# A shorter lead-in and the last weights rounded earlier, in a fused attention and mixer kernel

## The chip, the cores and the metric

The kernel runs on one core of a Trainium2 chip. A core has five engines that run side by side[...]: TensorE (PE, matrix products and transposes), VectorE (DVE), ScalarE (ACT), GpSimd (POOL) and SyncE (SP), which here only issues transfers. Data come from HBM by DMA into SBUF; TensorE writes its results to PSUM. The metric is the device time of one execution in microseconds, the median of the runs.

## The reference

Attention in which a query sees only the keys of its own cluster, and behind it an MLP mixer, in float32:

```python
# q, k, v: (4, 8, 768, 64); centroids: (8, 16, 64)
q_n, k_n, c_n = q / |q|, k / |k|, centroids / |centroids|      # norms + 1e-6
q_assign = argmax(q_n @ c_n.T);  k_assign = argmax(k_n @ c_n.T)
mask   = q_assign[:, :, :, None] == k_assign[:, :, None, :]
scores = where(mask, q @ k.T / 8, -1e9)
attn   = softmax(scores) @ v
x  = attn.transpose(0, 2, 1, 3).reshape(4, 768, 512)
u  = x + (relu(x^T @ w_tok1) @ w_tok2)^T      # over the tokens: 768 -> 256 -> 768
out = u + relu(u @ w_ch1) @ w_ch2             # over the channels: 512 -> 1536 -> 512
```

## The kernel before

The heads are worked on in 16 pairs (`g`), each in six iterations (`m`), 96 in all. While pair `g` is computed, the clusters of pair `g + 1` are found (the routing): `q` and `k` are turned in blocks of 32, multiplied by the normed centroids, turned back, compared with their maximum, and the one-hot rows turned into `ohT`. The product of the one-hots is added to the scores in PSUM and does the masking.

The lead-in does all that for pair 0, with nothing beside it:

```python
def centroids_norm(cen):
    ...                                     # ss = sum of squares, lo = max(ss, 2**-100)
    nrm = small.tile([P, 1], F32, name="nrm0")
    nc.scalar.sqrt(nrm, lo)                 # L243
    for it in range(2):                     # two Newton steps, L246 to L252
        ... reciprocal, scalar_tensor_tensor, tensor_scalar on VectorE
    ...                                     # reciprocal, scaling (cn), turn on TensorE (pc),
                                            # copies to cnT and cnd (L257 to L267)

def begin():
    cen = small.tile([P, D], F32, name="cen")
    nc.sync.dma_start(cen, centroids.rearrange("h c d -> (h c) d"))
    load(0, (nc.scalar, nc.sync))           # q issued by ScalarE, k by SyncE; four transfers each
    make_identity(nc, ident)
    ...
    load(1)
    centroids_norm(cen)
    turn(0)                                 # two 128x768 turns on VectorE, k then q (L276)
    route_products(0)                       # pr, four f32 products of q and k together (L287)
    route(0)                                # sim, mx, oh on VectorE (L301 to L307)
    for a in (1, 0):
        route_turn(0, a)                    # six turns on TensorE, copy to ohT by ScalarE
```

A float32 product stands in the trace as two matmul records; that is why `pr` has eight.

The weights are rounded in steps. A step takes one piece of up to 128x512 and has two operations on ScalarE, three on VectorE and an integer addition on GpSimd; transfer, ScalarE's part and the rest of a piece lie in three steps that follow each other:

```python
def scalar_part(p):
    nc.scalar.activation(out=p["h"]..., in_=p["hi"]..., func=ACT.Abs)              # L193
    nc.scalar.activation(out=p["up"], in_=p["lo"], func=ACT.Copy, scale=2.0**-29)  # L195
def rest(dst, p):
    nc.vector.tensor_scalar(...)            # L200, max and min
    nc.vector.tensor_scalar(...)            # L205, mask and shift
    nc.vector.scalar_tensor_tensor(...)     # L210
    nc.gpsimd.tensor_tensor(...)            # L217
```

The loop over the iterations, and what comes behind it:

```python
begin()
weights = list(weight_steps(stage, W, ("tok1", "tok2", "ch1")))
ends = [...]                                # 32 token products: tok1 (two per batch), tok2 (six)
for m in range(last + 5):                   # last = 96
    g, s = divmod(m, GROUPS)                # GROUPS = 6
    ...                                     # outputs, sums, scores, values of the pair
    if g < NPAIR - 1:
        ...                                 # the routing of pair g + 1, one part at each s
    if s == 1 and g + 2 < NPAIR:
        load(g + 2)
    if m % WEVERY == 0 and weights:         # WEVERY = 4
        weights.pop(0)()
    ...
    if m >= last:
        for _ in range(2):
            if ends:
                ends.pop(0)()               # ten of the 32
attention.close()
W["ch2"] = ...
beside = list(left_weights())               # four sums of 128x1536 on VectorE (w1s, L474)
beside += weight_steps(pool("mstage", 2, staging), W, ("ch2",))   # 12 pieces, 14 steps
while ends:                                 # the other 22
    for _ in range(-(-len(beside) // len(ends))):
        beside.pop(0)()
    ends.pop(0)()
    if len(ends) in (11, 9):
        turn_u(0, len(ends) == 9)           # turns x to uT; at 9 also four differences (uTs)
```

`tok2` writes a PSUM tile (four buffers in `ps_m`), and VectorE adds it to `x` and frees it:

```python
def tok2(b, j):
    pu = mtile([P, DM], "pu")
    for t in range(NT):
        nc.tensor.matmul(pu, lhsT=W["tok2"][:, t, j], rhs=h1s[b][:, t], ...)     # L460
    nc.vector.tensor_tensor(out=xs[b][:, j], in0=pu, in1=xs[b][:, j], op=ALU.add) # L463
```

Behind that come the channel products (L584 and L635, seven products in place of eight), which take the second half of the time.

Of the kernel before, what the change touches and what calls it, by code (L numbers as in the profile page):

```python
# [8 lines left out]
F32 = mybir.dt.float32  # L9
BF16 = mybir.dt.bfloat16  # L10
# [36 lines left out]
def kernel(  # L47
# [46 lines left out]
    wc1pool = pool("wc1pool", 1)  # L94
    tokens = fast.enter_context(ExitStack())
    tokpool = pool("tokpool", 1, tokens)
    attention = fast.enter_context(ExitStack())
    loads = pool("loads", 2, attention)
# [4 lines left out]
    stage = pool("stage", 2, attention)  # L103
    pools = {}


# [5 lines left out]
    ohs = [small.tile([P, 2, NJ, P], BF16, name=f"oh{i}", bufs=1) for i in range(2)]  # L112
    rcps = const.tile([P, 2 * NPAIR, 2, HJ], F32, name="rcps")
    cells = const.tile([P, NPAIR], F32, name="cells")

# [10 lines left out]
    def load(g, queues=None):  # L126


        b, f = divmod(g, NF)
        st = state.setdefault(g, {})  # L130
        st["qk"] = loads.tile([P, 2, NJ, NQ, QP], F32, name="qk")
        st["va"] = loads.tile([P, 2, NJ, D], F32, name="va", bufs=3)
# [99 lines left out]


    def centroids_norm(cen):
        sq = small.tile([P, D], F32, name="censq")
        ss = small.tile([P, 1], F32, name="ss")
# [3 lines left out]
        lo = small.tile([P, 1], F32, name="lo")  # L240
        nc.vector.tensor_scalar_max(out=lo, in0=ss, scalar1=float(2.0**-100))
        nrm = small.tile([P, 1], F32, name="nrm0")
        nc.scalar.sqrt(nrm, lo)  # L243
        for it in range(2):
            rr = small.tile([P, 1], F32, name="rr")
            nc.vector.reciprocal(out=rr, in_=nrm)  # L246
            tw = small.tile([P, 1], F32, name="tw")
# [3 lines left out]
            nrm = small.tile([P, 1], F32, name="nrm")  # L251
            nc.vector.tensor_scalar(  # L252
                out=nrm, in0=tw, scalar1=0.5, scalar2=(1e-6 if it else 0.0),
                op0=ALU.mult, op1=ALU.add,
            )
        rden = small.tile([P, 1], F32, name="rden")
        nc.vector.reciprocal(out=rden, in_=nrm)  # L257
        cn = small.tile([P, 2, D], F32, name="cn")
        for i in range(2):
            nc.vector.tensor_scalar_mul(out=cn[:, i], in0=cen, scalar1=rden)  # L260
        pc = ps_w.tile([P, H * C], F32, tag="w", name="pc")
        nc.tensor.transpose(out=pc, in_=cn.rearrange("p i d -> p (i d)"), identity=ident)
        nc.vector.tensor_copy(out=cnT, in_=pc)
        nc.vector.memset(cnd, 0.0)
        for i in range(2):
            rows = slice(i * D, (i + 1) * D)
            nc.vector.tensor_copy(  # L267
                out=cnd[rows, :, i], in_=cnT.rearrange("p (f i c) -> p f i c", f=NF, i=2)[rows, :, i]
            )


    def turn(g):
        st = state[g]
        st["T"] = qktp.tile([P, 2, NJ, P], F32, name="qkT")
        for a in (1, 0):
            nc.vector.transpose(  # L276
                out=st["T"][:, a].rearrange("p j t -> p (j t)"),
                in_=st["qk"][:, a].rearrange("p j i d -> p (j i d)"),
            )

    def route_products(g):

        st, f = state[g], g % NF
        pr = ps_w.tile([P, 2, NJ, QP], F32, tag="w", name="pr")
        for i in range(NQ):
            rows = slice(i * QP, (i + 1) * QP)
            nc.tensor.matmul(  # L287
                pr[rows], lhsT=cnd[:, f].rearrange("p i c -> p (i c)"),
                rhs=st["T"][:, :, :, rows].rearrange("p a j r -> p (a j) r"),
                start=True, stop=True,  # L290
            )
        st["pr"] = pr

    def route(g):

        st = state[g]
        NR = 2 * NJ * 2
        sc = small.tile([P, NR, C], F32, name="sim")  # L300
# [3 lines left out]
        mx = small.tile([P, NR], F32, name="mx")  # L304
        nc.vector.reduce_max(out=mx, in_=sc, axis=AX.X)
        oh = ohs[g % 2].rearrange("p a j (h x) -> p (a j) h x", h=2)[:, :, :, 0:C]
        nc.vector.tensor_tensor(  # L307
            out=oh, in0=sc.rearrange("p (n h) c -> p n h c", h=2),
            in1=mx.rearrange("p (n h) -> p n h", h=2).unsqueeze(3).to_broadcast([P, 2 * NJ, 2, C]),
            op=ALU.is_ge,  # L310
        )
# [167 lines left out]
    def left_weights():  # L479

        w = W["ch1"]
        half = DCH // 2
        A = {
            f"A{i + 1}{j + 1}": w[:, 2 * j : 2 * j + 2, half * i : half * i + half]
            for i in range(2)
            for j in range(2)
        }
        extra = pools["wsums"].tile([P, 3, 2, half], F32, name="w1s")
        A["S1"], A["S2"], A["S4"] = (extra[:, i] for i in range(3))
        yield lambda: add(A["S1"], A["A21"], A["A22"])  # L490
# [191 lines left out]


    def begin():
        cen = small.tile([P, D], F32, name="cen")
# [4 lines left out]
        nc.vector.memset(ones, 1.0)  # L690
# [7 lines left out]
        for a in (1, 0):  # L698
            route_turn(0, a)

    begin()
    weights = list(weight_steps(stage, W, ("tok1", "tok2", "ch1")))
# [12 lines left out]
    for m in range(last + 5):  # L715
# [37 lines left out]
    assert not weights and not state  # L753
    attention.close()
    other = fast.enter_context(ExitStack())
    W["ch2"] = pool("wc2pool", 1, other, side="right").tile([P, NCT, DM], F32, name="wc2")
    pools["wsums"] = pool("wsums", 1, other, side="right")
    pools["u"] = pool("upool", 1, other, side="right")
    staging = ExitStack()
# [238 lines left out]
```

## Time and profile before

| | |
|---|---|
| time, median of 3 runs | 924.56 us (924.08 to 924.62) |
| span of the profiled execution | 919.6 us |
| TensorE busy | 892.4 us, 97% |
| VectorE busy | 507.0 us, 55% |
| ScalarE busy | 309.6 us, 34% |
| first score product | 16.45 us after the start |
| first channel product (pX, L584) | 465.5 us after the start |

An engine's busy time is summed over its instructions. "PE" is the matmuls and "PEld" the loading of their stationary operand. A row of the timeline gives the start in us, the length, engine and line, operation, and tiles; what stands in brackets is the time that the engine was idle before, and what ended it. Busy shares are means over stages with different limits, so the stages are looked at one by one below.

### The profile page before, as it was taken

What the parts mean: (1) busy time and instruction counts of PE and PEld (TensorE: products, weight loads), DVE (VectorE), ACT (ScalarE), POOL (GpSimd) and SP (SyncE); (2) the same over time, 40 slices, a digit from 0 to 9 for tenths busy, and PEclk for the clock granted to TensorE, in tenths of its full rate; (3) what the DMA queues carried; (4) which work ended last, traced back from release to release, by engine and by line L of the source; (5) the groups of instructions that cost most, each with busy time, mean ns of one, the idle gap of its engine ahead of it and who ended that gap; (6) DMA issues with size and microseconds to landing.
All of it is one profiled execution on the core that took longest, in us unless ns stands there. A gap on an engine that the chain in (4) does not pass through costs nothing.

```text
span 919.6 us, 11532 instructions
## 1 busy us (share of the span) xinstructions
PE 892.4 (97%) x4563; PEld 524.2 (57%) x4563; DVE 507.0 (55%) x842; ACT 309.6 (34%) x517; POOL 48.5 (5%) x40
## 2 busy tenths in 40 slices
PE   4999999999999999999999899999999999999997
PEld 1444444444444444444457668677686776868676
DVE  4778787878787865147865344342443334433342
ACT  3565555656565555103521031210212112130210
POOL 1010100101010100002310000000000000000000
PEclk9999999999999999999999999999999999999999
DMA  8343435243434110002400000000010000100001
GB/s 173 75 99 84 92 77 110 66 110 84 96 87 76 43 48 1 1 0 75 132 0 1 1 0 35 35 0 1 1 46 23 1 1 0 58 12 1 0 13 60
DMA packets 112829, 41.74 MB, mean 45 GB/s; under 512 B 101632, under 2 KB 105728, under 8 KB 112768
## 3 DMA queue, kind: packets, MB, share of 16 engines
q1 hardware_dynamic: 109632, 40.55, 18.0%
q10 hardware_dynamic: 3136, 0.39, 0.3%
q8 instruction: 37, 0.61, 0.3%
q14 instruction: 24, 0.20, 0.1%
HBM read 34.64 MB, written 6.29 MB: 45 GB/s over the span
## 4 chain that ended last, share of the span: by engine, by line
PE 95%; DVE 3%; ACT 1%; issue 0%; ACTq 0%; DVEq 0%
PE sc L349 18%; PE av L378 15%; PE pX L635 14%; PE pX L584 14%; PE pZ L635 7%; PE pZ L584 7%; PE ph L451 5%; PE pY L635 3%; PE pY L584 3%; PE pu L460 3%; PE px L413 2%; PE po L325 2%; PE pr L287 1%; PE den L394 1%; PE pt L523 1%; DVE wh L200 1%
## 5 line engine op out<-in xcount | busy, mean ns | idle before, releaser
L355 ACT ACTIVATE ex<-sc 128x768 f32<-128x768 f32 x192 | 145.3, 808 | 117.2 <-PE sc L349 117.2
L368 DVE TENSOR_TENSOR sum<-sum,ex 128x768 f32<-128x768 f32 x128 | 133.5, 1043 | 30.6 <-ACT ex L355 22.2
L378 PE MATMUL av<-ex,va 128*64 128x384 f32 x768 | 145.1, 499 | 0.0
L349 PE MATMUL sc<-qkT 64*128 64x384 f32 x768 | 140.6, 485 | 0.0
L378 PEld LDWEIGHTS av<-ex,va 128*64 128x64 f32 x768 | 46.6, 136 | 86.5 <-issue 82.7
L349 PEld LDWEIGHTS sc<-qkT 64*128 64x128 f32 x768 | 71.2, 188 | 31.8 <-issue 0.6
L584 PE MATMUL pX<-uT,wc 128*128 128x384 f32 x192 | 67.4, 487 | 1.6 <-issue 1.6
L592 ACT COPY p<-pX 128x384 f32<-128x384 f32 x24 | 11.4, 475 | 143.2 <-PE pX L584 143.2
L584 PEld LDWEIGHTS pX<-uT,wc 128*128 128x128 f32 x192 | 36.2, 190 | 26.4 <-issue 2.7
L217 POOL TENSOR_TENSOR wc<-wT,wup 128x512 int32<-128x512 int32 x24 | 35.3, 1470 | 290.8 <-DVE wT L210 182.3
L349 PE MATMUL sc<-ohT 64*128 64x384 bf16 x384 | 48.5, 329 | 1.7 <-ACT ohT L327 1.0
L460 PE MATMUL pu<-h,wt 128*128 128x512 f32 x96 | 43.1, 596 | 3.6 <-DVE x L463 3.6
L419 DVE TENSOR_TENSOR x<-px,rcps 128x384 f32<-128x384 f32 x32 | 17.8, 558 | 49.4 <-PE px L413 47.9
L451 PE MATMUL ph<-x,wt 128*128 128x512 f32 x96 | 42.1, 594 | 0.0
L477 DVE TENSOR_TENSOR c<-pZ,u 128x384 f32<-128x384 f32 x24 | 13.4, 558 | 46.8 <-PE pZ L584 46.8
L477 DVE TENSOR_TENSOR x<-pX,x 128x256 f32<-128x256 f32 x24 | 10.2, 424 | 51.3 <-PE pX L635 51.3
L477 DVE TENSOR_TENSOR hA<-pY,p 128x384 f32<-128x384 f32 x24 | 13.4, 557 | 40.7 <-PE pY L584 40.7
L635 PE MATMUL pX<-w2s,hA 128*128 128x256 f32 x144 | 35.1, 380 | 0.5 <-DVE x L477 0.5
L635 PE MATMUL pX<-wc,hA 128*128 128x256 f32 x144 | 35.0, 379 | 0.0
L635 PE MATMUL pZ<-w2s,hS 128*128 128x256 f32 x144 | 35.0, 379 | 0.0
L635 PE MATMUL pY<-wc,hA 128*128 128x256 f32 x144 | 35.0, 379 | 0.0
L635 PE MATMUL pX<-w2s,hS 128*128 128x256 f32 x144 | 35.0, 379 | 0.0
(111 smaller groups left out, 1209.3 us busy)
## 6 DMA issues: line engine op xcount, KB each, us to landing
raw<-in_moe_w_ch_dram SPq DMA_DIRECT2D x24, 512.0 KB, 3.9
qk<-in_k_dram SPq DMA_DIRECT2D x64, 96.0 KB, 4.4
va<-in_v_dram SPq DMA_DIRECT2D x16, 384.0 KB, 3.4
out_dram<-x SPq DMA_DIRECT2D x24, 256.0 KB, 2.0
qk<-in_q_dram SPq DMA_DIRECT2D x60, 96.0 KB, 3.1
raw<-in_moe_w_tok_dram SPq DMA_DIRECT2D x3, 512.0 KB, 5.1
raw<-in_moe_w_tok_dram SPq DMA_DIRECT2D x4, 384.0 KB, 3.5
qk<-in_q_dram ACTq DMA_DIRECT2D x4, 96.0 KB, 3.6
```

The lines of the kernel that those rows point to most:

```text
L217: nc.gpsimd.tensor_tensor(out=dst.bitcast(I32), in0=T, in1=up, op=ALU.add)
L325: nc.tensor.transpose(out=po[:, j], in_=oh[:, a, j], identity=identb)
L349: nc.tensor.matmul(scs[i][:, h, 0:HS], lhsT=src[rows, 1, j0 + i], rhs=src[rows, 0, js], start=start, stop=not start,)
L355: nc.scalar.activation(out=ex, in_=scs[i][:, :, 0:HS], func=ACT.Exp, scale=SM_SCALE)
L368: nc.vector.tensor_tensor(out=acc, in0=acc, in1=e[i], op=ALU.add)
L378: nc.tensor.matmul(st["av"][h * D : (h + 1) * D], lhsT=st["va"][:, h, j], rhs=ex[:, h], start=(j == 0), stop=(j == NJ - 1),)
L413: nc.tensor.transpose(out=px[:, i], in_=avT[:, i], identity=ident)
L451: nc.tensor.matmul(pf, lhsT=W["tok1"][:, j, t * P : (t + 1) * P], rhs=xs[b][:, j], start=(j == 0), stop=(j == NJ - 1),)
L460: nc.tensor.matmul(pu, lhsT=W["tok2"][:, t, j], rhs=h1s[b][:, t], start=(t == 0), stop=(t == NT - 1))
L477: nc.vector.tensor_tensor(out=dst, in0=a, in1=b, op=ALU.add)
L584: nc.tensor.matmul(psum, lhsT=A[a][:, k, c * P : (c + 1) * P], rhs=R[r][:, k], start=start and k == 0, stop=k == 1, skip_group_check=not s ...
L635: nc.tensor.matmul(psum, lhsT=h2[a][:, k, i * P : (i + 1) * P], rhs=Bw[w][:, 3 * part + k], start=start and k == 0, stop=k == 2, skip_grou ...
```

## The change

It has two parts. The first is to shorten the lead-in. The root of the norms is computed on VectorE, from a first guess out of the bits and one more Newton step, so that ScalarE needs no table for it; the table of the exponential is loaded at once, by an exponential that nothing uses. `k` is turned and routed ahead of `q`, so that the engines overlap, and `q`'s one-hots of pair 0 are copied by VectorE. Matmuls of zeros, whose result nothing reads, keep TensorE at work between the real ones.

The second moves the rounding of the last weights (`ch2`) forward: it begins with the last pair of heads, whose iterations have no next pair to route, and takes the place in SBUF that the routing leaves. For that, the routing's tiles get pools of their own at the right end of SBUF. What is rounded, and how, stays the same.

The core of the diff (renamed pools and the loops that only pass on `a0`, `a1` are left out):

```diff
@@ centroids_norm
-        nrm = small.tile([P, 1], F32, name="nrm0")
-        nc.scalar.sqrt(nrm, lo)
-        for it in range(2):
+        nrm = rsmall.tile([P, 1], F32, name="nrm0")
+        nc.vector.tensor_scalar(
+            out=nrm.bitcast(I32), in0=lo.bitcast(I32), scalar1=0.5, scalar2=float(0x1FBD1DF5),
+            op0=ALU.mult, op1=ALU.add,
+        )
+        for it in range(3):
@@ turn, route_products, route: for one of k and q alone
-    def turn(g):
+    def turn(g, kinds=(1, 0)):
-    def route_products(g):
+    def route_products(g, a0=0, a1=2):
-    def route(g):
+    def route(g, a0=0, a1=2):
@@ route_turn
         if a == 0:
-            nc.scalar.copy(out=st["ohT"][:, 0], in_=po)
+            if g == 0:
+                nc.vector.tensor_copy(out=st["ohT"][:, 0], in_=po)
+            else:
+                nc.scalar.copy(out=st["ohT"][:, 0], in_=po)
@@ begin
         load(0, (nc.scalar, nc.sync))
+        nc.vector.memset(ones, 1.0)
+        warm = rsmall.tile([P, WMAX], BF16, name="warm")
+        nc.vector.memset(warm, 0.0)
+        nc.scalar.activation(out=rsmall.tile([P, QP], F32, name="expd"), in_=ones, func=ACT.Exp)
         make_identity(nc, ident)
         ...
         load(1)
+        pw = ps_av.tile([P, HS], F32, name="av")
+        def keep_warm(n):
+            for _ in range(n):
+                nc.tensor.matmul(pw, lhsT=warm[:, 0:P], rhs=warm[:, P : P + HS], start=True, stop=True)
+        keep_warm(12)
         centroids_norm(cen)
-        turn(0)
-        route_products(0)
-        route(0)
-        for a in (1, 0):
-            route_turn(0, a)
+        keep_warm(7)
+        turn(0, (1,))
+        route_products(0, 1, 2)
+        turn(0, (0,))
+        route(0, 1, 2)
+        keep_warm(1)
+        route_products(0, 0, 1)
+        keep_warm(2)
+        route_turn(0, 1)
+        route(0, 0, 1)
+        keep_warm(1)
+        route_turn(0, 0)
@@ the loop
-        if m % WEVERY == 0 and weights:
+        if m == last - GROUPS:
+            assert not weights
+            routing.close()
+            W["ch2"] = pool("wc2pool", 1, side="right").tile([P, NCT, DM], F32, name="wc2")
+            weights = list(weight_steps(stage, W, ("ch2",)))
+        if (m % WEVERY == 0 if m < last - GROUPS else m % 2 or m > last) and weights:
             weights.pop(0)()
@@ behind the loop
-    beside = list(left_weights())
-    beside += weight_steps(pool("mstage", 2, staging), W, ("ch2",))
+    beside = weights + list(left_weights())
```

More of the change, by code (lines that the diff above doesn't have):

```diff
@@ L96 @@
     tokpool = pool("tokpool", 1, tokens)
+    staging = fast.enter_context(ExitStack())
+    stage = pool("stage", 2, staging)
     attention = fast.enter_context(ExitStack())
-    loads = pool("loads", 2, attention)
+    loads = pool("loads", 3, attention)
     small = pool("small", 2, attention)
@@ L102 @@
     sums = pool("sums", 2, attention)
-    stage = pool("stage", 2, attention)
+    routing = fast.enter_context(ExitStack())
+    qkpool = pool("qkpool", 2, routing, side="right")
+    rsmall = pool("rsmall", 2, routing, side="right")
     pools = {}
@@ L111 @@
     cnd = const.tile([P, NF, 2, C], F32, name="cnd")
-    ohs = [small.tile([P, 2, NJ, P], BF16, name=f"oh{i}", bufs=1) for i in range(2)]
+    ohs = [rsmall.tile([P, 2, NJ, P], BF16, name=f"oh{i}", bufs=1) for i in range(2)]
     rcps = const.tile([P, 2 * NPAIR, 2, HJ], F32, name="rcps")
@@ L130, in load @@
         st = state.setdefault(g, {})
-        st["qk"] = loads.tile([P, 2, NJ, NQ, QP], F32, name="qk")
-        st["va"] = loads.tile([P, 2, NJ, D], F32, name="va", bufs=3)
+        st["qk"] = qkpool.tile([P, 2, NJ, NQ, QP], F32, name="qk")
+        st["va"] = loads.tile([P, 2, NJ, D], F32, name="va")
         for a, src in ((1, k), (0, q)):
@@ L234, in centroids_norm @@
     def centroids_norm(cen):
-        sq = small.tile([P, D], F32, name="censq")
-        ss = small.tile([P, 1], F32, name="ss")
+        sq = rsmall.tile([P, D], F32, name="censq")
+        ss = rsmall.tile([P, 1], F32, name="ss")
         nc.vector.tensor_tensor(out=sq, in0=cen, in1=cen, op=ALU.mult)
         nc.vector.reduce_sum(out=ss, in_=sq, axis=AX.X)
-        lo = small.tile([P, 1], F32, name="lo")
+        lo = rsmall.tile([P, 1], F32, name="lo")
         nc.vector.tensor_scalar_max(out=lo, in0=ss, scalar1=float(2.0**-100))
-        nrm = small.tile([P, 1], F32, name="nrm0")
-        nc.scalar.sqrt(nrm, lo)
-        for it in range(2):
-            rr = small.tile([P, 1], F32, name="rr")
+        nrm = rsmall.tile([P, 1], F32, name="nrm0")
[4 more added lines that the diff above has]
+        for it in range(3):
+            rr = rsmall.tile([P, 1], F32, name="rr")
             nc.vector.reciprocal(out=rr, in_=nrm)
-            tw = small.tile([P, 1], F32, name="tw")
+            tw = rsmall.tile([P, 1], F32, name="tw")
             nc.vector.scalar_tensor_tensor(
@@ L250, in centroids_norm @@
             )
-            nrm = small.tile([P, 1], F32, name="nrm")
+            nrm = rsmall.tile([P, 1], F32, name="nrm")
             nc.vector.tensor_scalar(
-                out=nrm, in0=tw, scalar1=0.5, scalar2=(1e-6 if it else 0.0),
+                out=nrm, in0=tw, scalar1=0.5, scalar2=(1e-6 if it == 2 else 0.0),
                 op0=ALU.mult, op1=ALU.add,
             )
-        rden = small.tile([P, 1], F32, name="rden")
+        rden = rsmall.tile([P, 1], F32, name="rden")
         nc.vector.reciprocal(out=rden, in_=nrm)
-        cn = small.tile([P, 2, D], F32, name="cn")
+        cn = rsmall.tile([P, 2, D], F32, name="cn")
         for i in range(2):
@@ L269, in centroids_norm @@
             )
-    def turn(g):
+    def turn(g, kinds=(1, 0)):
         st = state[g]
-        st["T"] = qktp.tile([P, 2, NJ, P], F32, name="qkT")
-        for a in (1, 0):
+        if 1 in kinds:
+            st["T"] = qktp.tile([P, 2, NJ, P], F32, name="qkT")
+        for a in kinds:
             nc.vector.transpose(
@@ L279, in turn @@
             )
-    def route_products(g):
+    def route_products(g, a0=0, a1=2):
         st, f = state[g], g % NF
-        pr = ps_w.tile([P, 2, NJ, QP], F32, tag="w", name="pr")
+        pr = ps_w.tile([P, a1 - a0, NJ, QP], F32, tag="w", name="pr")
         for i in range(NQ):
@@ L288, in route_products @@
                 pr[rows], lhsT=cnd[:, f].rearrange("p i c -> p (i c)"),
-                rhs=st["T"][:, :, :, rows].rearrange("p a j r -> p (a j) r"),
+                rhs=st["T"][:, a0:a1, :, rows].rearrange("p a j r -> p (a j) r"),
                 start=True, stop=True,
@@ L292, in route_products @@
         st["pr"] = pr
-    def route(g):
+    def route(g, a0=0, a1=2):
         st = state[g]
-        NR = 2 * NJ * 2
-        sc = small.tile([P, NR, C], F32, name="sim")
+        NR = (a1 - a0) * NJ * 2
+        sc = rsmall.tile([P, NR, C], F32, name="sim")
         nc.vector.transpose(
@@ L303, in route @@
         )
-        mx = small.tile([P, NR], F32, name="mx")
+        mx = rsmall.tile([P, NR], F32, name="mx")
         nc.vector.reduce_max(out=mx, in_=sc, axis=AX.X)
-        oh = ohs[g % 2].rearrange("p a j (h x) -> p (a j) h x", h=2)[:, :, :, 0:C]
+        oh = ohs[g % 2][:, a0:a1].rearrange("p a j (h x) -> p (a j) h x", h=2)[:, :, :, 0:C]
         nc.vector.tensor_tensor(
             out=oh, in0=sc.rearrange("p (n h) c -> p n h c", h=2),
-            in1=mx.rearrange("p (n h) -> p n h", h=2).unsqueeze(3).to_broadcast([P, 2 * NJ, 2, C]),
+            in1=mx.rearrange("p (n h) -> p n h", h=2).unsqueeze(3).to_broadcast([P, NR // 2, 2, C]),
             op=ALU.is_ge,
@@ L684, in begin @@
     def begin():
-        cen = small.tile([P, D], F32, name="cen")
+        cen = rsmall.tile([P, D], F32, name="cen")
         nc.sync.dma_start(cen, centroids.rearrange("h c d -> (h c) d"))
         load(0, (nc.scalar, nc.sync))
+        nc.vector.memset(ones, 1.0)
+        warm = rsmall.tile([P, WMAX], BF16, name="warm")
+        nc.vector.memset(warm, 0.0)
+        nc.scalar.activation(out=rsmall.tile([P, QP], F32, name="expd"), in_=ones, func=ACT.Exp)
         make_identity(nc, ident)
         nc.gpsimd.tensor_copy(out=identb, in_=ident)
-        nc.vector.memset(ones, 1.0)
         for oh in ohs:
@@ L693, in begin @@
         load(1)
-        centroids_norm(cen)
-        turn(0)
-        route_products(0)
-        route(0)
-        for a in (1, 0):
-            route_turn(0, a)
+        pw = ps_av.tile([P, HS], F32, name="av")
[3 more added lines that the diff above has]
+        keep_warm(12)
+        centroids_norm(cen)
+        keep_warm(7)
[10 more added lines that the diff above has]
+        route_turn(0, 0)
     begin()
@@ L752 @@
                     ends.pop(0)()
-    assert not weights and not state
+    assert not state
     attention.close()
[L755 to L759, printed above, removed]
-    beside = list(left_weights())
-    beside += weight_steps(pool("mstage", 2, staging), W, ("ch2",))
+    pools["wsums"] = pool("wsums", 1, side="right")
+    pools["u"] = pool("upool", 1, side="right")
+    beside = weights + list(left_weights())
     while ends:
```

## The prediction

> **What bounds the kernel now.** I first read the page's engine shares. TensorE is busy for 892.4 of 919.6 us, so the kernel can only get shorter where TensorE stands still or runs slowly. I then cut the span into stretches (the table by windows; its columns are the length, then busy time and instruction count of PE, PEld, DVE, ACT and POOL, the granted clock, the DMA share and GB/s):
> ```profile
> PE 892.4 (97%) x4563; PEld 524.2 (57%) x4563; DVE 507.0 (55%) x842; ACT 309.6 (34%) x517; POOL 48.5 (5%) x40
> ...
> 0.00:16.45 16.45, 3.42 (x22) 1.68 (x23) 8.54 (x24) 3.11 (x6) 3.62 (x9) 1.00 0.88 178
> 16.45:22.80 6.35, 5.68 (x33) 2.71 (x33) 1.44 (x2) 4.19 (x5) 0.00 (x0) 1.00 0.90 152
> 22.80:370.00 347.20, 347.20 (x2510) 152.94 (x2508) 263.10 (x379) 201.36 (x303) 29.55 (x19) 1.00 0.34 76
> 370.00:445.30 75.30, 75.30 (x218) 34.09 (x215) 35.71 (x50) 15.85 (x29) 8.22 (x7) 1.00 0.14 42
> 445.30:465.70 20.40, 16.76 (x39) 6.74 (x38) 19.37 (x27) 5.97 (x10) 7.11 (x6) 1.00 0.25 77
> ```
> TensorE is full from 22.8 to 445.3 us. It is nearly idle in the first 16.45 us, and it loses some of the stretch from 445.3 to 465.7 us, where VectorE is busy for 19.37 of 20.40 us. The change touches just these two places, so each is read by itself.
>
> For the first, the timeline (start, length, engine and line, operation, tiles; in brackets the idle time before it and what ended it), with the rows that carry the chain:
> ```profile
> 3.64 1.28 ACT L243 ACT_TABLE_LOAD   x1 [3.64 <-issue]
> 5.17 0.16 DVE L246 RECIPROCAL rr<-nrm 128x1 f32<-128x1 f32 x1 [2.02 <-ACT nrm L243]
> ...
> 7.21 0.45 PE L262 MATMUL pc<-ident,cn 128*128 128x128 f32 x1 [7.21 <-DVE cn L260]
> ...
> 8.59 1.84 DVE L276 STREAM_TRANSPOSE qkT<-qk 128x768 f32<-128x768 f32 x2
> ...
> 10.48 1.51 PE L287 MATMUL pr<-qkT,cnd 128*32 128x384 f32 x8 [2.82 <-DVE qkT L276]
> ...
> 17.04 2.52 PE L349 MATMUL sc<-qkT 64*128 64x384 f32 x8
> ...
> 20.62 1.47 PE L349 MATMUL sc<-qkT 64*128 64x384 f32 x8
> ```
> The reader is to see three things: VectorE waits 2.02 us for a root on ScalarE, whose table load cannot start until ScalarE has issued q's transfers; everything behind it is one serial chain (norms, turn, products, route, turn of the one-hots, scores); and the same eight score matmuls take 2.52 us at 17.04 and 1.47 us at 20.62.
>
> For the second, the chain that ended last, in order of time:
> ```profile
> 457.14 0.60 DVE x L463
> 457.74 1.11 DVE wh L200
> 458.86 0.02 issue
> 458.88 0.44 DVE wh L205
> 459.32 0.04 DVEq L210
> 459.35 0.04 issue
> 459.40 0.69 DVE wT L210
> 460.09 0.60 DVE x L463
> ```
> This cycle of 2.95 us (457.14 to 460.09) frees one PSUM tile. TensorE fills one with four tok2 matmul records at 0.43 us each (a run of 24 took 10.30 us), so in 1.72 us. VectorE is the bound here, because a step of rounding the ch2 weights stands between two additions. The waits put it so:
> ```profile
> PE pu L460 <- DVE x L463: 3.6, 4, 1.0
> ```
>
> **What the Trainium skill says.** "TensorE: Matmul & The Clock Gate", Part 1: The HAM clock gate, says that TensorE runs at half rate until it has been busy for a window of about 3.4 us, and falls back after an idle one. The trace fits the first half: 0.315 us a score matmul (2.52/8) becomes 0.18 (1.47/8) after some 3 us of dense work. The window table's granted clock shows 1.00 all through, so durations are the evidence, not that column. "ScalarE: Activation LUTs", What ACT_TABLE_LOAD costs, gives 1283 ns; the two loads here took 1.28 us each (at 3.64 and 16.41). "DMA: Bandwidth & Descriptors", Issuing engines are not separate DMA queues, says that transfers of all queues share the same engines. The DMA share of 0.88 in the lead-in agrees, and so I expect k, the second half of a shared burst, to land no earlier than now. "SBUF — State Buffer", Who interferes with whom, says that a VectorE scalar operation in its two-port mode and a GpSimd operation block each other. The trace agrees: the first weight operation (L200) takes 0.42 us when it runs free and 1.18 us when it starts beside GpSimd's 1.27 us addition, so one rounding step costs VectorE 1.54 to 2.3 us.
>
> **Part 1, the lead-in.** *Root on VectorE.* The norm's first operation ends at 3.15 us, as now. Removed: the wait from 3.15 to 5.17. Added: a first guess (0.18 with the gap, as the 128x1 operation L252) and a third iteration. An iteration goes from 5.17 to 5.81, so 0.64 us. The three end at 3.17 + 0.18 + 3 x 0.64 = 5.27, where the two now end at 6.45. The rest is unchanged in length: to the end of cn 0.63, to the copy of pc 0.62, to the end of cnd 0.89. VectorE is then free at 7.41 instead of 8.59.
>
> *A new wait for k.* k's last transfer is issued at 3.66 and lands after 4.0 us (the view of tile qk), at 7.66; the last of q lands at about 7.2. Neither changes. So the turn of k starts at about 7.75, and of the 1.18 us freed by the root only 0.84 is kept.
>
> *k ahead of q.* A turn of one of them takes 0.925 us: k 7.75 to 8.67, q 8.67 to 9.6. TensorE makes k's products (half of the eight) beside q's turn. The route of one half starts at 9.62. A 192-column transpose out of PSUM (tile dent) takes 0.38 us where the 384-column one takes 0.58, so I take 0.38, 0.36 and 0.38 for the three operations and 0.13 of gaps: 1.25 us. k's route ends at 10.85, q's at 12.1. k's six transposes and ScalarE's copy with its accumulator (0.81 + 0.19) run beside q's route and end by about 12.4. After q's route: six transposes 0.5, and a VectorE copy of 768 columns, which I estimate at 0.95 from the transpose of as many, with handovers 0.1. The first scores start at 13.65 instead of 16.45: 2.8 us less.
>
> *Table and dummy matmuls.* The exp table is loaded behind q's issues, and the load at 16.41 goes; it lay beside the 3.12 us of cold scores, so alone it brings nothing. A dummy matmul has 384 columns; by the cold spacing of the TensorE page (columns over 1.2 GHz) I estimate 0.32 us for it, so twelve take 3.8 us, from about 1.2 to 5.0. pc is wanted at 5.9, so they delay nothing. Seven more take 1.1 us (warm) to 2.2 (cold) from 6.5 on, and k's products are due at 8.7. If TensorE is warm at 13.65, the first scores take 1.9 us and not 3.1, and the second exponential ends 3.2 us after their start where it now takes 3.95 (16.45 to 20.40). The second scores follow it at once and their last part is warm already (20.45 to 22.08). That brings about 0.75 us more, with some 0.15 us for products and transposes.
>
> Sum for the lead-in: 2.8 + 0.9 = **3.7 us**. Behind it lies a stretch in which TensorE never waits, so it should be kept whole. The turn of pair 1 needs q of pair 1, which lands at 11.0 + 3.7 = 14.7; TensorE asks for its products only at 18.4, so this wait stays hidden.
>
> **Part 2, the last weights.** Fourteen steps move forward: seven into the last pair of heads and the iterations after it, seven to the first seven of the 22 remaining token products, and the four VectorE sums of w1s (1.75 us each) behind them. All are over with the eleventh of the 22, just where the first u is turned. In 445.3 to 465.7 VectorE keeps four uTs differences (445.32 to 449.68, 4.4 us) and additions of 0.69 us per tile. Four PSUM buffers cover 4 x 1.72 = 6.9 us, more than the 4.4, so TensorE should run through. From 445.34 it has 36 records x 0.43 = 15.5 us to do and now takes until 465.67, 20.3 us. Gain: **4.8 us**, which agrees with 3.6 us of waits plus four restarts at 0.26 (1.98 instead of 1.72).
>
> Does it cost anything where it goes? In the last pair a step falls on every second iteration of about 3.6 us. VectorE owes the sums 1.74 us per iteration (five of about 1.04 in three), the outputs and reciprocals about 0.4, and 0.8 to 1.15 for half a step: 3.0 to 3.3 us. Routing, 3.64 us in six iterations (turn 1.95, then 0.58, 0.55 and 0.56), is missing there. In the token products after it, the tightest run is six tok2 tiles with five steps and one sum: VectorE needs some 17 us where TensorE needs 10.3, but four buffers and then two long tok1 tiles (12 records, 5.15 us each) lie behind it; my count by hand leaves no wait.
>
> Total: 924.56 - 3.7 - 4.8 = 916.06, rounded to 916.0.
>
> **The rivals.** (a) *The lead-in is bound by transfers.* If k landed later, because the first transfers differ between executions or the other traffic moves up, nearly the whole gain of the root would be lost: about 917. For it: a DMA share of 0.88; against it: nothing in the order of the transfers changes. (b) *The clock stays cold.* The gaps between the dummies are about 1 us, so an interrupted run may not count as busy. Then 0.9 us is lost, and a cold pair of dummies stands in front of k's transposes: 917 to 917.3. (c) *VectorE stays the bound of the transition.* If the moved steps let VectorE fall behind before the turns of u, its backlog reaches the same additions and half of the 4.8 us comes back: about 918.5. For it: 17 us of work against 10.3; against it: the two long tiles, and that TensorE shows no wait in the similar stretch before 445. (d) *The last pair is held up.* ScalarE gets 1.34 us of weight work (0.67 + 0.66 us) in every second iteration beside two exponentials of 0.81; should it delay the exponentials, three such iterations lose 1 us together: 917.
>
> **Range and chances.** Each part alone could miss by about a third: 2.3 to 4.8 us for the lead-in and 3.0 to 5.5 for the transition. Both ends together are unlikely, which gives 913.5 to 919.0. A gain of 2% would need 18.5 us, more than the lead-in and the transition hold together, and the parts that cost could hardly turn 8.5 us into a loss.
>
> **What would show it.** The timeline should have no ScalarE wait in the norms, the turn of k at 7.7 with a DMA as what ended the wait, the first scores at 13.6, and their f32 half in 1.5 us. The waits should list no tok2 tile behind the addition, and the first ch1 product should come 8 to 9 us earlier than at 465.5, with no new wait for tile den or sc in the last pair. The prediction is wrong if score matmuls at 13 us still take 0.31 us each, if the first scores begin after 15 us, or if the weight operation L200 still appears in the chain.

## The result, and the profile after

The changed kernel takes 917.04 us (median of four runs, 914.80 to 917.46) against 924.35 us: 7.3 us less, a ratio of 0.9916 (95% interval 0.9899 to 0.9933). The prediction was 916.0 with a range of 913.5 to 919.0.

The span of the profiled execution is 913.0 us. The table by stretches, cut where the changed kernel's stages end (first scores at 14.26 us, third scores at 19.35, last run of tok2 at 442.1, first channel product at 457.6), has the columns of the table before:

```profile
0.00:14.26 14.26, 9.36 (x52) 4.21 (x53) 8.75 (x32) 2.41 (x4) 3.62 (x9) 0.88 1.04 142
14.26:19.35 5.09, 4.47 (x32) 2.02 (x32) 3.25 (x4) 2.83 (x4) 0.00 (x0) 1.00 1.09 237
...
442.10:457.60 15.50, 15.50 (x38) 6.89 (x37) 8.86 (x12) 0.59 (x2) 0.00 (x0) 1.00 0.00 1
457.60:913.00 455.40, 445.70 (x1754) 326.98 (x1753) 178.76 (x361) 79.13 (x168) 0.00 (x0) 0.99 0.04 15
```

VectorE is busy for 8.86 of 15.50 us in the stretch of the last token products, where it had been busy for 19.37 of 20.40. The granted clock, 1.00 in every stretch of the kernel before but its last few us, is 0.88 in the lead-in. The timeline shows what became of the start (L285, L296 and L361 are the lines L276, L287 and L349 of the kernel before):

```profile
8.68 1.84 DVE L285 STREAM_TRANSPOSE qkT<-qk 128x768 f32<-128x768 f32 x2 [1.47 <-DMA qk<-in_k_dram]
9.71 0.87 PE L296 MATMUL pr<-qkT,cnd 128*32 128x192 f32 x8 [2.26 <-DVE qkT L285]
...
14.26 0.50 PE L361 MATMUL sc<-ohT 64*128 64x384 bf16 x4 [0.65 <-DVE ohT L337]
...
14.58 1.47 PE L361 MATMUL sc<-qkT 64*128 64x384 f32 x8
```

The wait for the root is gone, and a wait of 1.47 us for the transfer of k stands in its place: the turn of k begins at 8.68 us, where the turns had begun at 8.59. The first scores still come 2.19 us earlier, and they are warm, that is, at the full clock (1.47 us and not 2.52). That was a near thing. In stretches of 3 us the granted clock is

```profile
9.00:12.00 3.00, 2.29 (x18) 0.64 (x19) 2.73 (x6) 0.00 (x0) 0.00 (x0) 0.57 1.31 153
12.00:15.00 3.00, 2.35 (x23) 1.75 (x23) 2.33 (x5) 0.90 (x2) 0.00 (x0) 0.86 0.98 136
```

and in stretches of 0.5 us it falls to half at about 9.4 us, while TensorE waits for k, and is back at about 12.8, 1.4 us before the first scores. The products of k between these times ran cold (0.87 us for eight records).

In the chain that ended last, the tok2 run behind the turns of u is one piece:

```profile
442.15 15.45 PE pu L472 x36
457.60 1.29 PE pX L596 x4
```

These are the same 36 records that took from 445.34 to 465.67 before.

The sum can be read off three marks in the two traces. The first tok1 product moves from 373.03 to 369.68 us: 3.35 us for the lead-in. From there to the first channel product it is 87.92 instead of 92.64 us: 4.72 us for the weights. From there to the end it is 455.40 instead of 453.93 us: 1.47 us are lost in code that the change doesn't touch. The chain shows where. First the kernel after, then the kernel before, at the pause in which the range test (`fits`) reads its counts into registers:

```profile
513.37 1.34 issue
514.71 2.90 PE pX L596 x4
```

```profile
521.50 1.33 issue
522.83 1.53 PE pX L584 x4
```

The four records behind the pause take 2.90 us instead of 1.53. The table by stretches of the kernel after gives the reason in its third column from the end, the granted clock:

```profile
515.00:517.00 2.00, 2.00 (x4) 1.09 (x4) 0.00 (x0) 0.00 (x0) 0.00 (x0) 0.50 0.00 0
```

Behind 3.7 us of almost idle TensorE (511.02 to 514.71, with 0.19 us of work in it) the clock is at half for some 3 us. That is no effect of the change: the profiled execution of the kernel before happened to be spared. It took 921.37 us where the timed runs took 924.1 to 924.6, and among 26 more runs of that kernel the three with a mean clock of 0.999 took 921.5 us, the others, at 0.995 to 0.997, 923.0 to 924.7. Seven of the twelve traces of this document have the pause as it stands here; behind it the clock is at half for 3.4 us in six of them (the changed kernel, e1, e2, e3, e5, e8) and stays up only in that of the kernel before. So medians are compared with medians here, and a difference of two single traces has to leave such a drop out.

### The profile page after: what moved, and what is told of

Its sections match the earlier page's. It is cut to its first block, busy times and chain, and to the rows that moved or that the text cites. A ratio compares the mean times of both kernels' runs of the same rounds, so it can differ in the third digit from the quotient of the medians.

```text
span 913.0 us, 11598 instructions
## 1 busy us (share of the span) xinstructions
PE 897.8 (98%) x4594; PEld 527.4 (58%) x4594; DVE 506.1 (55%) x851; ACT 306.9 (34%) x515; POOL 48.4 (5%) x40
## 4 chain that ended last, share of the span: by engine, by line
PE 98%; DMA 1%; DVE 0%; issue 0%; ACT 0%
PE sc L361 18%; PE av L390 15%; PE pX L596 14%; PE pX L647 14%; PE pZ L647 7%; PE pZ L596 7%; PE ph L463 5%; PE pu L472 5%; PE pY L647 3%; PE pY L596 3%; PE px L425 2%; PE po L334 2%; PE pr L296 1%; PE den L406 1%; PE pt L535 1%; DMA qk<-in_k_dram 1%
## 5 line engine op out<-in xcount | busy, mean ns | idle before, releaser
L361 PE MATMUL sc<-qkT 64*128 64x384 f32 x768 | 139.5, 482 | 0.0
L361 PEld LDWEIGHTS sc<-qkT 64*128 64x128 f32 x768 | 70.5, 187 | 31.4
L604 ACT COPY p<-pX 128x384 f32<-128x384 f32 x24 | 11.4, 475 | 153.0 <-PE pX L596 153.0
L361 PE MATMUL sc<-ohT 64*128 64x384 bf16 x384 | 48.2, 328 | 1.3 <-DVE ohT L337 0.6
L472 PE MATMUL pu<-h,wt 128*128 128x512 f32 x96 | 42.0, 592 | 0.0
L647 PE MATMUL pZ<-wc,hS 128*128 128x256 f32 x144 | 35.0, 379 | 0.0
```

The lines of the kernel that those rows point to most:

```text
L361: nc.tensor.matmul(scs[i][:, h, 0:HS], lhsT=src[rows, 1, j0 + i], rhs=src[rows, 0, js], start=start, stop=not start,)
L647: nc.tensor.matmul(psum, lhsT=h2[a][:, k, i * P : (i + 1) * P], rhs=Bw[w][:, 3 * part + k], start=start and k == 0, stop=k == 2, skip_grou ...
```

## The experiments

The theory after the result: (1) the two parts are independent; (2) the lead-in is bound by the landing of k and by whether the clock is up when the first scores run; (3) both kernels lose 4 to 5 us at the range test, a pause and a drop of the clock. The rivals stand with each experiment. "First tok1" is the start of the first tok1 product, by which all of the lead-in's gain has been made.

### The lead-in alone (e1)

```diff
-        if m == last - GROUPS:
-            ... weights = list(weight_steps(stage, W, ("ch2",)))
-        if (m % WEVERY == 0 if m < last - GROUPS else m % 2 or m > last) and weights:
+        if m % WEVERY == 0 and weights:
...
-    beside = weights + list(left_weights())
+    beside = list(left_weights()) + list(weight_steps(stage, W, ("ch2",)))
```

> The changed kernel with the last weights rounded where the kernel before rounds them: the lead-in part alone. Theory (the parts are independent, and the changed kernel loses time elsewhere, to a slower TensorE clock behind the pause for the range test, the function fits): the second scores end near 18.6 us instead of 22.1, the wait of tok2 for the addition stays at 3.6 us, and the time is 924.4 - 3.5 = 920.9 us, or 1.5 to 3 us more where the clock drops behind that pause. Rival (the two parts share a gain, the lead-in being given back later in the attention): 923 to 924 with the clock at its full value throughout.

Measured: 920.98 us against 924.51 for the kernel before, timed beside it, 3.5 us less (ratio 0.9960, interval 0.9946 to 0.9974; these two stand in brackets below, too). The waits of TensorE show tok2 behind the addition as before:

```profile
PE pu L472 <- DVE x L475: 3.7, 4, 1.0
```

The second scores ended at 20.2 us, not at 18.6. The timeline has two reasons:

```profile
6.40 2.45 PE L714 MATMUL av<-warm 128*128 128x384 bf16 x7
9.10 1.84 DVE L285 STREAM_TRANSPOSE qkT<-qk 128x768 f32<-128x768 f32 x2 [1.60 <-DMA qk<-in_k_dram]
```

k was waited for until 9.10 us, 0.42 us later than in the first trace of the changed kernel. And the dummies didn't warm TensorE at all here: the seven behind the first twelve took 0.35 us each (1.30 us for all seven in the first trace), and everything up to the first scores, which began at 15.23 us, ran cold. That is the larger share of the 1.6 us. The time fits the theory; the miss lies with k and with the clock.

### The weights alone (e2)

The lead-in of the kernel before (root on ScalarE, both turned together, no dummies) with the moved weights.

```diff
-        nc.vector.tensor_scalar(out=nrm.bitcast(I32), ...)
-        for it in range(3):
+        nc.scalar.sqrt(nrm, lo)
+        for it in range(2):
...
-        keep_warm(12)
         centroids_norm(cen)
-        ...
+        turn(0)
+        route_products(0)
+        route(0)
+        for a in (1, 0):
+            route_turn(0, a)
```

> The changed kernel with the lead-in of the kernel before: the moved weights alone. Theory: the last tok2 run is 15.45 us without a wait, the first channel product comes 4.6 to 4.9 us earlier than the kernel before has it (461 us after the start), and the time is 919.6 us, or 1.5 to 3 us more where the clock drops behind the pause for the range test. Rival (the steps in the last pair of heads hold up its scores): the stretch of the last pair is longer by 1 to 2 us and the gain is 3 us or less, 921.5 us.

Measured: 919.37 us against 924.51, 5.1 us less (0.9947, 0.9931 to 0.9964). The chain has the same single run (L466 here is L472 of the changed kernel):

```profile
446.35 15.45 PE pu L466 x36
```

The rival is out: in the changed kernel's chain the last pair takes 25.94 us from its first scores (343.74) to the first tok1 (369.68), and 25.93 (347.10 to 373.03) in the kernel before, so the steps moved there cost nothing. In this trace even the old lead-in waits for k, until 8.95 us:

```profile
8.95 1.84 DVE L282 STREAM_TRANSPOSE qkT<-qk 128x768 f32<-128x768 f32 x2 [0.40 <-DMA qk<-in_k_dram]
```

The two parts give 3.5 and 5.1 us alone, 8.6 together, and the changed kernel gives 7.3 against the kernel before and 8.1 when both were timed again (e8); within the spread of the runs they add up.

### The dummies taken out (e3)

```diff
-            for _ in range(n):
+            for _ in range(0):
                 nc.tensor.matmul(pw, lhsT=warm[:, 0:P], ...)
```

> The changed kernel without its 23 dummy matmuls. Theory (they pay by the clock alone): the first eight f32 score records take 2.5 us instead of 1.47, products and transposes of pair 0 take up to twice as long, and the time is 1.3 to 2 us more than that of the changed kernel, about 918.5 us. Rival (the dummies only delay the chain, or make the transfer of k land at 8.6 instead of 7.7): k lands earlier and the time is the same or lower, 915 to 917.

Measured: 917.22 us (0.9920, 0.9903 to 0.9937), 7.3 us below the kernel before, as the changed kernel's 917.04 is, and with runs closer together (916.55 to 917.52). The trace shows the cold products that theory expected:

```profile
9.16 1.84 DVE L285 STREAM_TRANSPOSE qkT<-qk 128x768 f32<-128x768 f32 x2 [1.70 <-DMA qk<-in_k_dram]
...
15.56 2.79 PE L361 MATMUL sc<-qkT 64*128 64x384 f32 x8
```

The first tok1 comes at 372.36, 2.7 us later than in the trace of the changed kernel; 0.5 us of that is a later landing of k, and 2.0 lie behind the start of the first scores. So the dummies don't delay k, and against that one trace they pay; but the medians say that they often don't. That led to e8.

### TensorE kept busy at the range test (e4)

```diff
+        fill = ps_w.tile([P, P], F32, tag="w", name="fill")
+        stay(24)                 # nc.tensor.matmul(fill, lhsT=identb, rhs=identb, ...)
         pn = ps_w.tile([1, 3], F32, tag="w", name="pn")
         nc.tensor.matmul(pn, lhsT=ones[:, 0:1], rhs=good, start=True, stop=True)
+        stay(20)
```

> The changed kernel with 44 extra matmuls of 128 columns around the small product of the range test (the function fits), so that TensorE isn't idle while it waits for the test. Theory (the 3.7 us of idling there bring the clock to half for some 3 us, in some executions and not in others): no stretch at 0.50 behind the test, the ch1 product behind it takes 1.5 us instead of 2.9, all runs agree within 0.5 us, and the time is about 913.5 us. Rival (the spread of the changed kernel's times, 914.8 to 917.5, comes from the lead-in or from transfers): the spread stays and the time is 916 to 917.

Measured: 914.45 us (913.85 to 916.21; 0.9898, 0.9882 to 0.9915). No stretch behind the test lies below 1.00 any more, up to the last few us of the kernel. Against the kernel before, timed beside it, that is 10.1 us, where the changed kernel has 7.3 (8.1 in e8): 1.9 to 2.8 us more. But the spread stayed, where theory had 0.5 us, with one run at a mean clock of 1.000 (913.85) and one at 0.994 (916.21). So the pause at the test is one of two places where the clock falls between the start and the last few us; the trace shows the other in the lead-in (0.82 from 9 to 12 us, 0.61 from 12 to 15).

### k ahead of q in the transfers (e5)

```diff
         for a, src in ((1, k), (0, q)):
-            queue = queues[a] if queues else nc.sync
             for c in range(NQ):
+                queue = queues[c % 2] if queues else nc.sync
```

> The changed kernel with the first load spread otherwise: SyncE and ScalarE each issue two of k's four transfers and then two of q's, so that k is ahead of q in the transfers too and not only in VectorE's order. Theory (the wait for k, 7.21 to 8.68 us in the changed kernel's trace, bounds the lead-in, and its length differs between executions): the turn of k begins at 7.3 to 7.5, the turn of q waits for q instead, to about 8.7, the scores begin about 0.9 us earlier than after a turn of k at 8.68, and TensorE's pause between the dummies and k's products is shorter than 1.2 us, so that the clock isn't lowered in it. Time 1 to 2 us below the changed kernel in the same call. Rival (all eight transfers share the engines and end together, so k ends no earlier): no difference.

Measured: 914.17 us (912.57 to 915.86) against 923.62 for the kernel before and 915.48 for the changed one (e8), timed beside it; the ratios to the kernel before, 0.9903 (0.9885 to 0.9920) and 0.9916 (0.9902 to 0.9930), overlap, so the times alone don't show a gain. The trace does:

```profile
7.42 0.98 DVE L285 STREAM_TRANSPOSE qkT<-qk 128x768 f32<-128x768 f32 x1
...
9.00 0.98 DVE L285 STREAM_TRANSPOSE qkT<-qk 128x768 f32<-128x768 f32 x1 [0.60 <-DMA qk<-in_q_dram]
```

k's turn begins at 7.42 with no wait, q's waits 0.60 us for q and begins at 9.00, where q's turn began at about 9.6 in the changed kernel. First tok1 at 368.80, the earliest of all traces. The wait for k was real; what the reorder leaves is the wait for the last of the eight transfers.

### The range test split (e6)

```diff
-        pn = ps_w.tile([1, 3], F32, tag="w", name="pn")      # in fits()
+        return good
+    def fits_count(good):          # called behind the next ch1 chunk (i == 0)
+        pn = ...                   # product and counts
+        return count
+    def fits_load(count):          # called two ch1 chunks later (i == 2)
+        loaded = [nc.values_load(...)]
```

> The changed kernel with the range test (the function fits) in three places: VectorE's operations where they are now, the small product and the counts one ch1 chunk later, the reading of the counts into registers two ch1 chunks after that. Theory (TensorE idles 3.7 us there and then runs at half clock for about 3 us): the waits lose pn behind good (1.9 us) and most of the 1.6 us of issue, no stretch at 0.50 follows, and the time is 4 to 5 us below the changed kernel, near 912.5 us. Rival (the pause only moves to where the registers are read, as each engine must wait there for the counts): 1.5 to 2 us below it.

Measured: 910.67 us (910.23 to 911.20; 0.9864, 0.9847 to 0.9880), 4.8 us below the changed kernel timed beside it (e8). The chain runs through the place where the pause had been:

```profile
521.48 0.12 PE pn L686 x2
521.60 2.78 PE pX L596 x8
```

Neither pn nor the reading of the registers ends a wait of TensorE any more. The rival, that the pause would only move, is out.

### Both (e7), and more dummies (e9)

e7 has the edits of e5 and e6.

> Both edits, k first in the transfers and the range test in three places. Theory (they touch different pauses and add up): 5 to 7 us below the changed kernel, near 911 us. Rival (both gains are the same clock effect and only one of them can be had): no more than with the split test alone.

Measured: 908.63 us (908.44 to 911.23; 0.9843, 0.9828 to 0.9857), 6.9 us below the changed kernel timed beside it (e8), 2.0 below e6, and the lowest of all. Four runs at a mean clock of 0.999 or 1.000 took 908.4 to 909.1; the profiled one, at 0.995, took 911.23, with the f32 half of the first scores cold:

```profile
14.57 2.79 PE L361 MATMUL sc<-qkT 64*128 64x384 f32 x8
```

e9 fills the pauses of its lead-in:

```diff
-        keep_warm(7)              # in front of k's products
+        keep_warm(11)
-        keep_warm(1)              # in front of q's products
+        keep_warm(6)
-        keep_warm(2)              # in front of k's transposes
+        keep_warm(3)
-        keep_warm(1)
+        keep_warm(3)
         route_turn(0, 0)
+        keep_warm(6)
```

> The kernel with k first and the split range test, with more dummy matmuls in the pauses of the lead-in: 11 instead of 7 in front of k's products, 6 instead of 1 in front of q's, 3 for 2, 3 for 1, and 6 more behind q's transposes, in front of the first scores. Theory (the clock falls again when the lead-in leaves TensorE idle for about half of some 3 us, which then costs 2 to 3 us): the f32 half of the first scores takes 1.5 us, no stretch of the lead-in lies below 1.00 behind the first dummies, and the time is 908.0 to 908.6 us with no run above 909.5. Rival (the extra dummies stand in the way of the real products, or the drop has nothing to do with idling): 909 to 911 us, with some runs at a clock of 0.995.

Measured: 909.41 us (908.98 to 910.36; 0.9844, 0.9831 to 0.9858). The clock was 0.998 or more in all five runs, and the trace has no stretch below 1.00 in the lead-in:

```profile
14.47 1.45 PE L361 MATMUL sc<-qkT 64*128 64x384 f32 x8
```

The time is no better than e7's, though, and above the 908.0 to 908.6 expected, with one run above 909.5: the last six dummies run from 13.06 to about 14.1 and stand in front of the first scores. These begin at 14.13, 0.31 us after VectorE's copy of q's one-hots ends at 13.82; in e5 they follow it after 0.05. Theory and rival each have a share. That dummies in the way cost some 0.3 us is shown. That idling brings the drop is shown at the range test, where none of the five traces with the pause filled or split has it (e4, e6, e7, e9, e10) and six of the seven others do; in the lead-in five runs without a drop agree with it, but e7 had only one drop in five.

### Both without any dummy (e10)

e7 with the edit of e3.

> The same kernel (k first, split range test) without any dummy matmul. Theory (dummies pay 2 us where the clock then stays up): products, transposes and first scores run at half rate, the f32 half of the first scores takes 2.5 to 2.8 us, and the time is 910.5 us, 2 us above the 908.6 us of the kernel with its 23 dummies. Rival (they pay nothing on balance): 908.5 to 909.

Measured: 910.29 us (910.09 to 911.02; 0.9855, 0.9840 to 0.9870), 1.7 us above e7's median, which was not timed beside it, and 0.9 above e9's, which was; the intervals of the ratios overlap. The f32 half of the first scores took 2.24 us, less than expected, since the clock came up while they ran. With k early and the test split, the dummies pay 0.9 to 1.7 us, near what theory said.

### The changed kernel once more (e8)

> The changed kernel itself once more, in the same call as the three before it. Theory (what differs between its executions is where k lands, 7.7 to 9.2 us, and whether the clock drops while TensorE waits for k and behind the range test): 915 to 917.5 us, and below the 917.2 us of the kernel without dummies by 1 us or more in its lowest runs but by less in its median. Rival (the dummies bring nothing): 917.2 us in the median.

Measured: 915.48 us (915.17 to 916.68), 8.1 us below the kernel before, timed beside it (0.9916, 0.9902 to 0.9930). The median lies in theory's range; the kernel without dummies (e3) is 7.3 us below its own, and the intervals overlap. The trace of e8 is of a less lucky execution than the first one. In the timeline the seven dummies are warm and the scores cold again, and the table by stretches has the clock between:

```profile
6.18 1.30 PE L714 MATMUL av<-warm 128*128 128x384 bf16 x7
...
14.94 2.79 PE L361 MATMUL sc<-qkT 64*128 64x384 f32 x8
```

```profile
12.00:15.00 3.00, 2.35 (x19) 1.63 (x19) 2.01 (x5) 0.90 (x2) 0.00 (x0) 0.50 1.08 140
```

Seven dummies in 1.30 us are 0.19 us each, warm. Then TensorE idles for 2.35 us until k has been turned, and 1.5 us later, at about 11.4, the clock falls to half until about 18 us. Set side by side, the traces say what the clock is worth. From the first scores to the first tok1 it is 355.42 us where they are warm (changed kernel 14.26 to 369.68, e5 13.38 to 368.80) and longer where they are cold: 356.58 in the kernel before, 356.96 in e8, 357.40 in e3, 357.42 in e7. That is 1.2 to 2.0 us (0.4 to 1.0 in e6, e1 and e10, where the clock came up during the first scores), and it differs from execution to execution of the same kernel.

## Why the prediction was right, and where its steps were off

**The range held, and both places were right.** The gain came from the lead-in and from the last token products, and from nowhere else. Measured alone the parts give 3.5 and 5.1 us; the prediction had 3.7 and 4.8. (By difference, the lead-in is left with 2.2 to 3.0 of the changed kernel's 7.3 to 8.1.)

**The weights: right step by step.** 36 records in one run of 15.45 us (predicted 15.5), no wait behind the addition, nothing lost in the last pair (25.94 against 25.93 us), and the four differences of uTs are covered by the four PSUM buffers. Rivals (c) and (d) are out.

**The lead-in: the sum came near, three terms in it did not hold.**

- *The landing of k.* The step took k's landing from one trace, 3.66 + 4.0 us, and said that it wouldn't change. In the changed kernel the last transfer of k took 4.7 us and was issued at 3.9, and in six other traces with this load order (e1, e2, e3, e4, e6, e8) the same transfer took 5.0 to 5.4. Of the 0.84 us that the root was to bring, nothing was kept: the turn of k begins at 8.68, 0.09 us later than before, and with the root still on ScalarE (e2) it waited for k as well. This is rival (a), that the lead-in is bound by transfers; it had a price of 1 us in the prediction, and e5 confirms it.
- *From the turn of k to the scores.* Predicted 5.90 us, measured 5.58. It is 7.86 in both traces of the old lead-in (before, e2) and 5.80 in e3, which has the new order and no dummies; so nearly all that the scores gained is the new order of k and q with VectorE's copy. No run takes these two apart, nor the early table from the rest. The products of k took 0.87 us, being cold in that execution (0.53 in e5), but VectorE's copy of q's one-hots took 0.56 us and not the 0.95 estimated from a float32 transpose. The estimate overlooked the bf16 operand. The Trainium skill's "VectorE: DVE Perf Modes", Why PSUM operands drop a tier, would have told: a PSUM operand still allows the mode of two 16-bit elements a cycle. 768 at two a cycle of 0.96 GHz, the page's clock, are 0.40 us, an estimate, and 0.80 at one; the 0.56 us measured lie between, so more than one a cycle went through.
- *The clock.* Cold scores were priced at 0.75 us in what follows them; they cost 1.16 us in the kernel before (356.58 - 355.42) and up to 2.0 elsewhere. And the prediction took "warm" for a state that lasts once reached. Rival (b) said that gaps of about 1 us might count as idling; the pause turned out to be 2.3 us, as k came late, and in the changed kernel, e4, e6, e7 and e8 the clock fell in the lead-in after it had been up; in e1 it came up only with the first scores. So the dummies' gain is a matter of chance as the kernel stands (917.04 with, 917.22 without), and 0.9 to 1.7 us where k is early and the test split.

2.19 us for the earlier scores and 1.16 us for warmer ones make the 3.35 us of the two traces. That this comes so near to 3.7 is partly luck: the clock was back in time in that execution, and in e8 the first tok1 comes at 371.31, only 1.72 us earlier than in the trace of before. Two of the signs by which the prediction called itself wrong also turn up, though not in the first trace: in e8 the first f32 score matmuls take 0.35 us each (2.79 for eight), and in e1 and e6 the first scores begin after 15 us (15.23 and 15.32). Late transfers of k and cold scores meet the kernel before as well: with its lead-in, e2 has the first tok1 at 373.88, 2.57 us later than e8.

**What the prediction did not have** is the range test. Its pause of 3.7 us was in the profile of before, in the waits and in the chain, and stayed there; that the clock falls behind it (in six of seven traces) could not be seen in that one trace, where it hadn't. It moves a difference of two single traces by 1.4 us but the difference of medians hardly, since both kernels have it.

That k lands later in most executions than in the profiled one of before is shown by seven traces; why is not settled. The SyncE issues took 3.31 us instead of 3.06 for the four, which explains 0.25 us of it in the changed kernel; in e6 they took 3.12 and the last transfer 5.4, the longest of all, so the rest lies in the transfers themselves.

## What to carry to other kernels

Before pricing a step that frees an engine, look up when its next input lands, and over several executions if you can: a serial chain moves only to the next wait. A matmul unit that is kept warm has to be kept warm up to the moment it counts; dummies in front of a pause may buy nothing. And a pause of a few microseconds on the bounding engine can cost more than its length: splitting a test so that its result is read long after it is made brought 4.8 us for a few lines, about as much as either part of the change.

## What the runs showed of the hardware

- The clock of TensorE falls to half after less than a wholly idle stretch (times from stretches of 0.5 us): in the changed kernel at about 9.4 us, TensorE having been idle since 7.45; in e8 at about 11.4, after 2.35 us idle and 1.5 us of work; in e7 at about 12.4, although no pause since 7.6 us was longer than 1.14 us (e5, with pauses of at most 0.82 us there, stayed up). It falls, too, around the end of the pause of 3.7 us at the range test, with 0.19 us of work in it. It stayed low for 3.4 us there, and in the lead-in for 3.4 (changed kernel, e4) or 6.8 us (e6, e7, e8). "TensorE: Matmul & The Clock Gate", Part 1 of the Trainium skill, speaks of one idle window of about 3.4 us; the cases in the lead-in are under that.
- The granted clock in the profile reads 1.00 from the start, although the first dummies run cold (twelve in 4.02 us, 0.33 each, against 0.19 for the next seven). So a cold start has to be read from durations.
- Where counts have just been made and are read into registers, TensorE stands still for 1.6 us, 1.3 of them after the counts are done; read two chunks after the making, they cost it no wait at all (e6).
- The same transfer in the same place of the program took 4.0, 4.7, 5.0, 5.1, 5.2 and 5.4 us in different executions.
